# Fourteen gather tiles instead of eight at the start of a talking-heads attention and feed-forward kernel

## The chip, the cores and the metric

The kernel runs on one core of a Trainium2 chip. The metric is the device time of one execution in microseconds (us). The program is built once; nothing is computed on the host. A core has five engines that run their own instruction streams in order and wait for one another by semaphores: TensorE (PE, matrix products; PEld in a profile is its weight load), VectorE (DVE), ScalarE (ACT), GpSimd (POOL) and SyncE (SP, which here only issues transfers). Sixteen DMA engines move data; transfers are issued from the queues of SP, ACT and POOL.

## The reference

Inputs are q, k, v of shape 8 batches x 12 heads x 448 positions x 64, two 12 x 12 matrices that mix heads before and after the softmax, and two feed-forward weights (768 x 2048 and 2048 x 768).

```python
scores = scale * np.matmul(q, k.transpose(0, 1, 3, 2))
scores = np.einsum('bhij,hg->bgij', scores, w_pre)
attn = np.exp(scores - np.max(scores, axis=-1, keepdims=True))
attn = attn / (np.sum(attn, axis=-1, keepdims=True) + 1e-09)
attn = np.einsum('bhij,hg->bgij', attn, w_post)
out = np.matmul(attn, v)              # to 3584 rows x 768
h = np.maximum(out @ w_in, 0.0)
return (h * h @ w_out).astype(np.float32)
```

## The kernel before

**Stages.** For each batch, q and k are loaded into a staging tile (`load_third`, L78, three thirds of q and three of k), turned on PE and copied to `qT` and `kT` (`turn_unit`, L157). `score_pair` (L306) computes the scores of two heads for a block of 128 query rows; ACT casts one head and DVE the other into the block's tile `S` (L320), of which there are three. A block is two "halves" of 64 rows; a batch has seven halves. `half_of` (L300) says which half a query row lies in, `halves` (L303) which halves a block has. With the "+1" of L301 block 0 holds one half (rows 0 to 63 of batch 0), block 1 the next two, and so on.

**Gather.** To mix heads, PE needs heads on the partitions. `gather` (L333) copies ten queries of all twelve heads from `S` into a gather tile `G` (120 rows of 448 numbers, 105 KB) with one DMA, or two where the ten queries lie in two blocks. There are 45 such steps for a batch, 360 in all, and eight tiles `G` (L129), used in turn (L337). The transfers go out on SP's queue, but for steps 1 and 3, which go out on ACT's.

**The main loop** (L487) takes two steps at a time; it is called a double step here, numbered `ds` from 0 to 179. In one double step: `mix(ds)` (L348) multiplies the two gather tiles by `pre`, ACT takes the exponential and its row sums (L359), DVE the reciprocal (L361), POOL scales to `d` (L363). Two double steps later (`LAG`) `unmix` (L374) multiplies by `post` with 32 small products and DVE casts to `at` (L391). `scores_for` (L465) issues one or two score pairs, as far ahead as `AHEAD` + `LEAD` say, and `gathers_for` (L474) issues gathers up to step 2 ds + 8. `spin` (L410) is products without use that run in the first ten double steps.

**Feed-forward.** `av_unit` (L175) multiplies the attention by v and writes `xt`. `ffn1_unit` (L229) makes `h_ps` from `xt` and the first weights; then a rectifier writes `hr` and a square writes `h2`. Batches after the first go through with all 448 columns at once, rectified on ACT and squared on POOL. Batch 0 goes in three parts of 160, 160 and 128 columns (L517 to L519); there every odd unit is rectified and squared on DVE, and every even one on ACT and POOL (L242 to L246). `hr` has two buffers. `ffn2_unit` (L261) multiplies by the second weights and stores. These units are filler: they are put between the mixes of later double steps by `fill` (L401), and what is left after the last mix runs at the end.

**Loads.** All loads are issued from POOL's queue, in front of the `d` of a certain double step (`at_load`, L430; the number is in steps, so half of it is the double step). Before the loop: q and k of batch 0, a quarter of `w1` and half of v of batch 0. Then the rest of `w1` in double steps 1 to 4, q and k of batch 1 in 4 to 9, the eight pieces of `w2` (four tiles `w2_0` to `w2_3`, two pieces each) in 10 to 17, v of batch 1 in 22 and 23, q and k of batch 2 in 23 to 28. In the built program a load waits for the semaphore of the eighth load before it, and a gather for that of the eighth gather before it: there are eight semaphores for each kind.

The order on PE and POOL is that of the program text (`manual_schedule`, L420).

Of the kernel before, what the change touches and what calls it, by code (L numbers as in the profile page):

```python
# [9 lines left out]
BF16 = mybir.dt.bfloat16  # L10
F32 = mybir.dt.float32
ACT = mybir.ActivationFunctionType
# [3 lines left out]
B, H, S, D = 8, 12, 448, 64  # L16
DMODEL = H * D
DFF = 2048
NPAIR = H // 2
FT = DFF // 128  # L20
R = 7
PR = S // R
# [8 lines left out]
LAG = 2  # L31
AHEAD = 6
LEAD = 14
OFF = 64 - H * (IQ // 2)
SCALE = 1.0 / 8.0
FIRST_TURN = (15, 16, 17)
# [6 lines left out]
def kernel(  # L43
# [11 lines left out]
    nc = tc.nc  # L55
    P = nc.NUM_PARTITIONS

    consts = ctx.enter_context(tc.tile_pool(name="consts", bufs=1))
    wts = ctx.enter_context(tc.tile_pool(name="wts", bufs=1))
# [6 lines left out]
    def bank(name, dtype=F32):  # L66
        return psp.tile([P, 512 if dtype == F32 else 1024], dtype, name=name, tag="ps")
# [29 lines left out]

    col_pre = wcol(w_pre, "col_pre", nc.sync, (OFF, 64))
    col_post = wcol(w_post, "col_post", nc.scalar, (0, 64))

    def stripes(name, p0s):
        t = consts.tile([P, HQ], F32, name=name)
        for p0, c0 in zip((0, 64), p0s):
# [4 lines left out]

    stripe_pre, stripe_post = stripes("stripe_pre", (OFF, 64)), stripes("stripe_post", (0, 64))
    pre = consts.tile([P, 64], BF16, name="pre")  # L110
    nc.vector.memset(pre[:, :], 0.0)
    nc.vector.tensor_tensor(out=pre[:, 0:HR].rearrange("p (i g) -> p i g", g=H),
                            in0=stripe_pre[:, :].unsqueeze(2).to_broadcast([P, HQ, H]),
# [12 lines left out]
    for t in dts:  # L126
        nc.vector.memset(t[:, S:DW], 0.0)

    gts = [work.tile([P, S], BF16, name=f"G{x}") for x in range(AHEAD + 2)]  # L129
    for t in gts:  # L130
        nc.vector.memset(t[0:OFF, :], 0.0)

    attn = [atp.tile([P, VS, H, TW], BF16, name=f"at{x}") for x in range(2)]
    for t in attn:
# [3 lines left out]
    cgblk = consts.tile([P, NPAIR], F32, name="cgblk")  # L138
    wpost_bf = consts.tile([H, H], BF16, name="wpost_bf")
    w1 = [wts.tile([P, NPAIR, DFF // 4], BF16, name=f"w1_{x}") for x in range(4)]  # L140
    w2 = [wts.tile([P, FT // 4, DMODEL], BF16, name=f"w2_{x}") for x in range(4)]

    qTs, kTs, bvecs, xts, h2ts, ats = {}, {}, {}, {}, {}, {}

# [78 lines left out]
    def load_w2(x):  # L223
        n = DFF // 8
        c = x % 2 * 2
        nc.gpsimd.dma_start(out=w2[x // 2][:, c:c + 2, :],
                            in_=moe_w_out[n * x:n * x + n, :].rearrange("(c p) m -> p c m", p=P))

    def ffn1_unit(b, ft, half, c0=0, c1=S):  # L229
        if half == 0:  # L230
            h_open[0] = bank("h_ps")
        ps = h_open[0]
        n = c1 - c0
        for c2 in range(3 * half, 3 * half + 3):
            nc.tensor.matmul(ps[:, 0:n], lhsT=w1[ft // 4][:, c2, ft % 4 * 128:ft % 4 * 128 + 128],  # L235
                             rhs=xts[b][:, c2, c0:c1], start=(c2 == 0), stop=(c2 == NPAIR - 1))
        if half == 0:
            return
        if (b, ft) not in h2ts:
            h2ts[(b, ft)] = ffnp.tile([P, S], BF16, name="h2", tag="h2", bufs=FT + 1)  # L240
        hr = ffnp.tile([P, S], F32, name="hr", tag="hr", bufs=2)
        if n < S and ft % 2:  # L242
            nc.vector.tensor_scalar_max(out=hr[:, 0:n], in0=ps[:, 0:n], scalar1=0.0)
        else:
            nc.scalar.activation(out=hr[:, 0:n], in_=ps[:, 0:n], func=ACT.Relu)  # L245
        square = nc.vector if n < S and ft % 2 else nc.gpsimd  # L246
        square.tensor_tensor(out=h2ts[(b, ft)][:, c0:c1], in0=hr[:, 0:n], in1=hr[:, 0:n], op=ALU.mult)  # L247

# [49 lines left out]
    Sb, Gs, dsb = {}, {}, {}  # L298

    def half_of(b, c):  # L300
        return R * b + c // PR + 1  # L301

    def halves(n):  # L303
        return [(z, *divmod(2 * n + z - 1, R)) for z in range(2) if 0 <= 2 * n + z - 1 < R * B]

    def score_pair(i):  # L306

# [22 lines left out]
    def needs(s):  # L330
        return NPAIR * (span_of(s)[1] + 1)

    def gather(k):  # L333

        b, t = steps[k]
        c, end = IQ * t, min(IQ * t + IQ, S)
        g = gts[k % len(gts)]  # L337
        eng = nc.scalar if k in (1, 3) else nc.sync
        row = OFF
        while c < end:  # L340
            n, z = divmod(half_of(b, c), 2)
            x = PR * z + c % PR
            m = min(end - c, P - x)
            eng.dma_start(out=g[row:row + H * m, :], in_=Sb[n][x:x + m, :, :])
            c, row = c + m, row + H * m
        Gs[k] = g
# [72 lines left out]
    steps = [(b, t) for b in range(B) for t in range(NT)]  # L419
    with tc.manual_schedule(engines={PE, POOL}):  # L420
# [9 lines left out]
        def at_load(i, f, *args):  # L430
            loads.setdefault(i, []).append(lambda: f(*args))
# [2 lines left out]
            at_load(-1, load_w1, x)  # L434
        for x in range(4):
            at_load(-1 if x < 2 else 2, load_v, 0, x)
            at_load(44 + x, load_v, 1, x)
        for x in range(2, 8):
            at_load(1 + x, load_w1, x)
        for x in range(6):  # L440
            at_load(9 + 2 * x, load_qk, 1, x)
            at_load(46 + 2 * x, load_qk, 2, x)
        for x in range(8):
            at_load(20 + 2 * x, load_w2, x)
        for b in range(1, B):
            if b + 2 < B:
                for x in range(6):
# [5 lines left out]
        issued, gathered = [NPAIR + 3], [0]  # L453
# [5 lines left out]
        def place(tile):  # L459
            blk = sum(tile >= x for x in starts) - 1  # L460
            if blk + 1 >= blocks:
                return NPAIR * blocks
            return NPAIR * (blk + (tile - starts[blk]) / (starts[blk + 1] - starts[blk]))

        def scores_for(ds, most):  # L465
            want = math.ceil(place(2 * ds + AHEAD + LEAD))
            full = sum(gathered[0] >= x for x in lasts)
            want = min(want, issued[0] + most, NPAIR * min(full + 3, blocks))
            want = max(want, needs(steps[min(2 * ds + 4, len(steps) - 1)]))
            while issued[0] < want and all(issued[0] % NPAIR < turned.get(x[1], 0) for x in halves(issued[0] // NPAIR)):  # L470
                score_pair(issued[0])
                issued[0] += 1

        def gathers_for(ds):  # L474
            while gathered[0] < min(2 * ds + AHEAD + 2, len(steps)):
                if issued[0] < needs(steps[gathered[0]]):
                    break
                gather(gathered[0])
                gathered[0] += 1
# [7 lines left out]
        for ds in range(nd + LAG):  # L487
            for i in (2 * ds, 2 * ds + 1):
                for f in loads.get(i, []):
                    f()  # L490
            now2 = steps[2 * ds:2 * ds + 2]
            old2 = steps[2 * (ds - LAG):2 * (ds - LAG) + 2] if ds >= LAG else []
            for b, t in now2:
                if t == 0:
                    if b == 0:
                        at_step(ds + 6, (100, cg_unit))
                    if b + 1 < B:
                        for x in range(3):
                            turns[ds + TURN.get(b, TURN[B])[x]] = (b + 1, x)
            rest = ((NT + 1) // 2 + LAG + 2 - ds) % (NT / 2) + 1  # L500
            if EARLY[2] < ds <= EARLY[2] + 2:
                rest = NT // 2
            elif ds <= EARLY[2]:
                rest = 1 + min(x for x in EARLY if x >= ds) - ds
            share = sum(w for w, _ in filler) / rest if now2 else 1e9
            now = timed.pop(ds, [])
            for w, f in now:
                f()
            if old2:
                unmix(ds - LAG)  # L510
                for b1, t1 in old2:
                    ends = PARTS[b1 % 2]
                    if t1 + 1 in ends:
                        part = ends.index(t1 + 1) - 1
                        for x, u in enumerate(av_units(b1, part)):
                            at_step(ds + (2 + x if b1 else 1), u)
                        if b1 == 0:  # L517
                            c = (IQ * ends[part], min(IQ * ends[part + 1], S))
                            at_step(ds + 1, (0, lambda c=c: filler.extend(ffn1_units(0, *c))))  # L519
                    if t1 == NT - 1:  # L520
                        if b1 > 0:
                            at_step(ds + 3, (0, lambda b1=b1: filler.extend(ffn1_units(b1))))
                        at_step(ds + (3 if b1 else 1), (0, lambda b1=b1: filler.extend(ffn2_units(b1))))
            if ds in turns:
                turn_unit(*turns.pop(ds), (nc.vector.tensor_copy, nc.scalar.copy))
                scores_for(ds, 0)
            else:
                behind = place(2 * ds + AHEAD + LEAD) - issued[0]
                scores_for(ds, 2 if behind > (2 if now else 1.5) else 1)
            if now2:  # L530
                mix(ds)
            gathers_for(ds)
            if ds < PARTS[0][1] // 2 + LAG:
                spin(4)
            if ds + 1 < nd + LAG:
                fill(share)
# [34 lines left out]
```

## Time and profile before

| what | us |
|---|---|
| median of 7 runs | 606.64 |
| lowest, highest of them | 603.52, 610.35 |
| the profiled execution's own time | 604.29 |
| its span, first to last instruction | 602.5 |
| PE busy in the span | 545.1 (90%) |
| DVE busy | 415.2 (69%) |
| ACT busy | 404.5 (67%) |
| POOL busy | 400.2 (66%) |
| exponentials of double step 3 start at | 32.68 |
| of double step 17 | 79.17 |
| of double step 31 | 123.37 |
| of double step 179, the last | 547.11 |

Times inside an execution count from the span's start. Two exponentials belong to each double step, so counting them in the timeline of ACT tells which double step runs when. The table's last four rows are read that way. From double step 31 to 179 one takes 2.86 us on average (423.74 / 148); from 3 to 17 it takes 3.32 us (46.49 / 14), from 17 to 31 it takes 3.16 us (44.20 / 14). After the last mix some 55 us of feed-forward are left. In every profile a line such as `G<-S` is named by the program's tiles: written from read.

### The profile page before, as it was taken

The page shows a single profiled execution, that of the slowest core. Times are in us where ns is not written, and L with a number is a line of the kernel's source. Part 1 is how long each engine was busy: PE and PEld are TensorE (multiplying, and loading weights), DVE is VectorE, ACT ScalarE, POOL GpSimd, SP SyncE. Part 2 cuts the span into 40 slices and gives each one's busy share as a digit, 9 for nine tenths or more (in the row PEclk, how much of TensorE's full clock was granted, in tenths as well). Part 3 has the DMA queues.
Part 4 walks back from the last instruction along what each step waited for, and adds up shares of the span by engine and source line. Part 5 has one row for each costly group of instructions (what it writes and reads, how often), then busy time and mean ns, then how long its engine had stood idle before and what let it go on. Part 6 is the DMA issues. An engine that isn't in the chain of part 4 may idle for free.

```text
span 602.5 us, 28176 instructions
## 1 busy us (share of the span) xinstructions
PE 545.1 (90%) x11810; PEld 308.8 (51%) x11810; DVE 415.2 (69%) x1068; ACT 404.5 (67%) x1199; POOL 400.2 (66%) x599
## 2 busy tenths in 40 slices
PE   3667688888999999999999999999999999999997
PEld 1434455654455456545555455545555555555554
DVE  5646689978786777776877677667877787755101
ACT  3546477677688867886678767876788767862420
POOL 5465758857559964798459954897468946882450
PEclk9879999999999999999999999999999999999999
DMA  9799967949755895479646885489553765442103
GB/s 141 118 220 181 200 130 123 188 62 196 153 123 114 147 158 127 98 129 150 144 105 104 150 162 114 89 149 152 126 114 68 123 151 122 77 80 58 37 10 83
DMA packets 83364, 74.98 MB, mean 124 GB/s; under 512 B 6436, under 2 KB 80164, under 8 KB 83236
## 3 DMA queue, kind: packets, MB, share of 16 engines
q1 hardware_dynamic: 51582, 49.35, 35.4%
q0 software_dynamic: 31264, 23.60, 29.2%
q8 instruction: 92, 1.51, 1.0%
q10 hardware_dynamic: 390, 0.22, 0.1%
q14 instruction: 36, 0.29, 0.1%
HBM read 47.20 MB, written 11.01 MB: 97 GB/s over the span
## 4 chain that ended last, share of the span: by engine, by line
PE 64%; DMA 11%; POOL 10%; DVE 6%; ACT 3%; issue 3%; ACTq 0%; DVEq 0%
PE o_ps L268 22%; PE h_ps L235 18%; DMA G<-S 11%; PE at_ps L386 8%; PE ot_ps L186 6%; PE m_ps L354 5%; POOL d L363 4%; POOL h L247 4%; DVE at L391 3%; PE s_ps L316 3%; POOL qkst L70 2%; PE tr_ps L169 2%; ACT e_sb L359 1%; ACT xt L197 1%; DVE h L247 1%
## 5 line engine op out<-in xcount | busy, mean ns | idle before, releaser
L363 POOL TENSOR_SCALAR d<-e_sb,rc 128x448 bf16<-128x448 f32 x360 | 226.5, 640 | 161.2 <-DVE rc L361 159.1
L391 DVE CAST at<-at_ps 128x480 bf16<-128x480 f32 x360 | 220.0, 651 | 54.6 <-PE at_ps L386 49.6
L359 ACT ACTIVATE e_sb<-m_ps 128x448 f32<-128x448 f32 x360 | 195.3, 556 | 39.4 <-PE m_ps L354 28.3
L235 PE MATMUL h_ps<-xt,w 128*128 128x448 bf16 (+2 forms) x960 | 163.0, 316 | 3.9 <-DVE at L391 2.7
L268 PE MATMUL o_ps<-w,h 128*128 128x384 bf16 (+1 forms) x1024 | 161.6, 328 | 0.1
L247 POOL TENSOR_TENSOR h<-hr 128x448 bf16<-128x448 f32 (+2 forms) x136 | 113.7, 844 | 17.1 <-ACT hr L245 17.1
L235 PEld LDWEIGHTS <-w 128*128 128x128 bf16 x960 | 79.0, 97 | 79.2 <-issue 30.1
L268 PEld LDWEIGHTS <-h 128*128 128x128 bf16 (+1 forms) x1024 | 82.4, 101 | 70.8 <-issue 25.4
L320 ACT CAST S<-s_ps 128x448 bf16<-128x448 f32 (+1 forms) x174 | 90.9, 539 | 38.2 <-PE s_ps L316 35.9
L354 PE MATMUL m_ps<-G,pre 64*64 64x448 bf16 x720 | 84.8, 358 | 28.4 <-DMA G<-S 21.7
L320 DVE CAST S<-s_ps 128x448 bf16<-128x448 f32 (+1 forms) x174 | 104.6, 614 | 0.1
L361 DVE RECIPROCAL rc<-sm 128x1 f32<-128x1 f32 x360 | 53.3, 158 | 64.8 <-ACT e_sb L359 61.9
L386 PEld LDWEIGHTS <-d 60*64 60x64 bf16 x5760 | 65.3, 109 | 56.3 <-issue 30.9
L386 PE MATMUL at_ps<-post,d 60*64 60x60 bf16 x5760 | 86.4, 195 | 7.9 <-POOL d L363 4.1
L245 ACT ACTIVATE hr<-h_ps 128x448 f32<-128x448 f32 (+2 forms) x136 | 68.3, 511 | 23.8 <-PE h_ps L235 13.0
L359 ACT ACTIVATION_READ_ACCUMULATOR e_sb<-m_ps 128x1 f32 x360 | 77.8, 216 | 0.0
L197 ACT ACTIVATE xt<-ot_ps,bvec 128x160 bf16<-128x160 f32 (+3 forms) x144 | 44.5, 385 | 46.8 <-PE ot_ps L186 36.3
L316 PE MATMUL s_ps<-kT,qT 64*64 64x448 bf16 x672 | 64.0, 364 | 0.3 <-ACT qT L173 0.2
L354 PEld LDWEIGHTS <-pre 64*64 64x64 bf16 x720 | 29.6, 106 | 49.4 <-issue 38.6
L275 DVE COPY osb<-o_ps 128x384 f32<-128x384 f32 x48 | 26.0, 548 | 39.3 <-PE o_ps L268 39.1
L186 PE MATMUL ot_ps<-at,v 128*64 128x160 bf16 (+4 forms) x1152 | 45.8, 230 | 1.4 <-DVE at L391 1.4
L186 PEld LDWEIGHTS <-v 128*64 128x64 bf16 x1152 | 38.4, 109 | 14.5 <-issue 13.8
(41 smaller groups left out, 215.4 us busy)
## 6 DMA issues: line engine op xcount, KB each, us to landing
G<-S SPq DMA_DIRECT2D x330, 105.0 KB
out_dram<-osb SPq DMA_DIRECT2D x48, 192.0 KB
v<-in_v_dram POOLq DMA_DIRECT2D x32, 192.0 KB, 5.4
qkst<-in_k_dram POOLq DMA_DIRECT2D x24, 224.0 KB, 6.0
qkst<-in_q_dram POOLq DMA_DIRECT2D x24, 224.0 KB, 5.9
w<-in_moe_w_in_dram POOLq DMA_DIRECT2D x8, 384.0 KB, 11.5
w<-in_moe_w_out_dram POOLq DMA_DIRECT2D x8, 384.0 KB, 7.7
out_dram<-osb SPq DMA_DIRECT2D x16, 96.0 KB
```

Of the source, the lines that this page charges most:

```text
L186: nc.tensor.matmul(ps[64 * hh:64 * hh + 64, TW * y + c0:TW * y + 2 + n], lhsT=vs[b][:, g, r, :], rhs=at[:, r, g, c0:2 + n], start=(y == 0 ...
L235: nc.tensor.matmul(ps[:, 0:n], lhsT=w1[ft // 4][:, c2, ft % 4 * 128:ft % 4 * 128 + 128], rhs=xts[b][:, c2, c0:c1], start=(c2 == 0), stop=( ...
L245: nc.scalar.activation(out=hr[:, 0:n], in_=ps[:, 0:n], func=ACT.Relu)
L247: square.tensor_tensor(out=h2ts[(b, ft)][:, c0:c1], in0=hr[:, 0:n], in1=hr[:, 0:n], op=ALU.mult)
L268: nc.tensor.matmul(dst, lhsT=h2ts[(b, ft)][:, mt * 128:mt * 128 + ROWS[mt]], rhs=w2[ft // 4][:, ft % 4, n2 * 384:(n2 + 1) * 384], start=(f ...
L316: nc.tensor.matmul(pss[hh][PR * z:PR * z + PR, 0:S], lhsT=qTs[b][rs, p, PR * j:PR * j + PR], rhs=kTs[b][rs, p, :], start=True, stop=True)
L320: copy(out=Sb[n][z0:z1, 2 * p + hh, :], in_=pss[hh][z0:z1, 0:S])
L354: nc.tensor.matmul(pss[y][64 * x:64 * x + 64, 0:S], lhsT=pre[rows, :], rhs=gs[x][rows, :], start=True, stop=True)
L359: nc.scalar.activation(out=e[:, :], in_=pss[y][:, 0:S], func=ACT.Exp, scale=SCALE, accum_out=sm[:, 0:1])
L363: nc.gpsimd.tensor_scalar(out=d[:, 0:S], in0=e[:, :], scalar1=rc[:, 0:1], scalar2=-1.0 / S, op0=ALU.mult, op1=ALU.add)
L386: nc.tensor.matmul(us[x][PR * z:PR * z + PR, c:c + HR], lhsT=d[rows, j:j + PR], rhs=post[rows, :], start=True, stop=True)
L391: nc.vector.tensor_copy(out=dst, in_=src)
```

## The change

Six more gather tiles are used for the first 28 steps. They are slices of the room in which the last quarter of the second weights (`w2_3`) is loaded later; the tile that the loads write is a second one of the same name and room. `gather_tile` picks the tile of a step, `gather_end` says how far gathers are issued: up to step 2 ds + 14 at first, up to step 36 in double steps 11 to 14, and up to 2 ds + 8 as before from then on. The score pairs follow `gather_end`.

The halves are numbered anew: block 0 now holds the first two halves of batch 0, so that the first twelve gathers read block 0 alone; half 7 is left empty, so that block 3 holds one half and all later blocks are as before. The number of score pairs is the same (174).

v of batch 1 is loaded in double steps 18 and 19, q and k of batch 2 in 20 to 25. The pieces of `w2` stay in double steps 10 to 17. All rectifiers run on ACT; the squares of the odd units of batch 0 stay on DVE.

```diff
+MORE = 6
+HEAD = 2 * (AHEAD + 2 + MORE)
...
+    shared = wts.tile([P, FT // 4 * DMODEL], BF16, name="w2_3", tag="w2_3", bufs=1)
     gts = [work.tile([P, S], BF16, name=f"G{x}") for x in range(AHEAD + 2)]
-    for t in gts:
+    more = [shared[:, S * x:S * x + S] for x in range(MORE)]
+    for t in gts + more:
         nc.vector.memset(t[0:OFF, :], 0.0)
+
+    def gather_tile(n):
+        if n < HEAD:
+            n = n % (AHEAD + 2 + MORE)
+            return more[n - AHEAD - 2] if n >= AHEAD + 2 else gts[n]
+        return gts[(n - HEAD) % (AHEAD + 2)]
+
+    def gather_end(ds):
+        return min(2 * ds + AHEAD + 2 + MORE, max(HEAD + AHEAD + 2, 2 * ds + AHEAD + 2))
...
-    w2 = [wts.tile([P, FT // 4, DMODEL], BF16, name=f"w2_{x}") for x in range(4)]
+    w2 = [wts.tile([P, FT // 4, DMODEL], BF16, name=f"w2_{x}") for x in range(3)]
...
+        if x == 6:
+            last = wts.tile([P, FT // 4 * DMODEL], BF16, name="w2_3", tag="w2_3", bufs=1)
+            w2.append(last[:, :].rearrange("p (c m) -> p c m", m=DMODEL))
...
-        if n < S and ft % 2:
-            nc.vector.tensor_scalar_max(out=hr[:, 0:n], in0=ps[:, 0:n], scalar1=0.0)
-        else:
-            nc.scalar.activation(out=hr[:, 0:n], in_=ps[:, 0:n], func=ACT.Relu)
+        nc.scalar.activation(out=hr[:, 0:n], in_=ps[:, 0:n], func=ACT.Relu)
...
-        return R * b + c // PR + 1
+        return R * b + c // PR + (b > 0)
...
-        return [(z, *divmod(2 * n + z - 1, R)) for z in range(2) if 0 <= 2 * n + z - 1 < R * B]
+        return [(h % 2, *divmod(h - (h > R), R)) for h in (2 * n, 2 * n + 1) if h != R and h <= R * B]
...
-        g = gts[k % len(gts)]
+        g = gather_tile(k)
...
-            at_load(44 + x, load_v, 1, x)
+            at_load(36 + x, load_v, 1, x)
...
-            at_load(46 + 2 * x, load_qk, 2, x)
+            at_load(40 + 2 * x, load_qk, 2, x)
         for x in range(8):
-            at_load(20 + 2 * x, load_w2, x)
+            at_load(21 + 2 * x, load_w2, x)
...
-            want = math.ceil(place(2 * ds + AHEAD + LEAD))
+            want = math.ceil(place(gather_end(ds) + LEAD - 2))
...
-            while gathered[0] < min(2 * ds + AHEAD + 2, len(steps)):
+            while gathered[0] < min(gather_end(ds), len(steps)):
...
-                behind = place(2 * ds + AHEAD + LEAD) - issued[0]
+                behind = place(gather_end(ds) + LEAD - 2) - issued[0]
```

## The prediction

> **What bounds the kernel now.** I read the page first, then the chain of waits in the opening, then the DMA queues and the engines stretch by stretch.
>
> ```profile
> span 602.5 us, 28176 instructions
> ...
> PE   3667688888999999999999999999999999999997
> ...
> DMA  9799967949755895479646885489553765442103
> ...
> PE 64%; DMA 11%; POOL 10%; DVE 6%; ACT 3%; issue 3%; ACTq 0%; DVEq 0%
> ```
>
> The first rows are busy tenths in 40 slices of 15 us. From the eleventh slice on PE is at 9, so there the end is set by PE's work, and neither its amount nor its order there changes: in the built program the products on PE stand in the same order from double step 31 on. Only the first 123 us, where PE has digits from 3 to 8, can give or lose time; whatever is gained by double step 31 (exponentials at 123.37) moves all the rest. DMA's digits are highest in just that part, and the chain has 11% of DMA, 66 us. The chain from 20 to 80 us says where:
>
> ```profile
> by line: DMA G<-S 80.4%; PE spin_ps L416 6.3%; PE m_ps L354 5.4%; PE h_ps L235 3.1%; issue 3.0%; PE at_ps L386 2.3%; PE s_ps L316 1.8%; PE tr_ps L169 1.1%; PE ot_ps L186 1.0%; ACT e_sb L359 0.7%; ACT hr L245 0.3%
> ...
> 26.96 9.15 DMA G<-S
> ...
> 37.63 11.35 DMA G<-S
> ...
> 50.31 10.76 DMA G<-S
> ...
> 63.12 11.97 DMA G<-S
> ```
>
> Each piece is one gather, from its issue to its landing; the first took 4.99 us (16.82 to 21.8). So gathers queue. In the two queues' shares (packets, MB, share of 16 engines), first in 18 to 24 us, when hardly a load runs, then in 25 to 61 us:
>
> ```profile
> q1 hardware_dynamic: 561, 0.47, 36.3%
> q10 hardware_dynamic: 260, 0.22, 12.3%
> ```
>
> ```profile
> q0 software_dynamic: 5010, 4.40, 80.2%
> q1 hardware_dynamic: 2728, 2.26, 24.2%
> ```
>
> q1 and q10 are the gathers of SP and ACT: 0.69 MB in 6 us, 1.07 tiles of 107.5 kB a us. Beside the loads (q0) it is 2.26 MB in 36 us, 0.58 tiles a us: 3.4 us for the two tiles of a double step, and the steps take 3.32. A piece of 11.35 us at 0.58 a us means 6.6 tiles waiting out of eight, so the gather queue is always full and the DMA engines are the limit, not the issue. Before that stretch SP itself stood still once:
>
> ```profile
> L344 SPq EVENT_SEMAPHORE  x3: 17/17/2072, 16.8 to 25.8; - x3
> ```
>
> 2.07 us between 22.0 and 24.17: the second part of gather 6 waits for the casts of block 1 (DVE S is the releaser), with all later gathers behind it in SP's queue and the DMA engines idle. The stages, columns us, PE, PEld, DVE, ACT, POOL busy, clock, DMA share, GB/s:
>
> ```profile
> 20.00:79.17 59.17, 39.98 (x1097) 26.93 (x1098) 36.71 (x98) 32.08 (x99) 39.32 (x62) 0.91 0.99 186
> 79.17:123.37 44.20, 36.78 (x1039) 26.45 (x1037) 40.51 (x108) 32.71 (x105) 31.76 (x56) 1.00 0.75 138
> 123.37:547.00 423.63, 410.50 (x9048) 222.41 (x9047) 316.07 (x803) 319.69 (x959) 304.56 (x447) 1.00 0.65 124
> ```
>
> In the second stage DVE is busy 40.51 of 44.20 us, 92%: it is the bound there. In the third PE has 97%.
>
> **The change, part by part.**
>
> *Block 0 full, more tiles: the head start.* The first twelve gathers now need block 0 alone. Its six pairs cost the same casts (one per head, 448 columns, 64 or 128 rows: 624 and 617 ns on DVE between 12 and 20 us), and eight products of full blocks took PE 0.72 us at 17.73 where four of the half block took 0.94 at 11.32, so gather 0 goes out at 16.82 as now. SP issues one each 0.87 us (16.82, 17.70, 18.56, 19.42; one takes 1.60), so gather 11 goes out at 16.82 + 9 x 0.87 + 0.8 = 25.4, where it goes out at 28.77 now. The cap of eight semaphores does not bite: gather 8 at 22.8 waits for gather 0, landed at 21.8. Loads start at 24.36 and move from about 26 on. By then about 6.7 tiles are moved now (6.4 issued before SP's stall, little after it); after, what goes out by 24.3, gathers 0 to 9, so 10. A lead of 3.3 tiles at 0.58 to 0.62 a us (0.62 is 24 tiles over the 39 us between the landings at 36.1 and 75.1) is worth 5.3 to 5.7 us. It lasts as long as loads and gathers share the engines. Lower end: if the engines only do the same work in another order, a tile is worth its packets, 126 x 51 ns / 16 = 0.40 us, 3.3 tiles 1.3 us. Upper end: the first double steps run at 2.2 us (22.23 to 26.68 for two); at that pace double step 6 comes at 35.6 where it is 43.23: 7.6 us. I take 5.5, nearest to the measured rate.
>
> *Fourteen deep afterwards.* At most eight are in flight, by the semaphores, and 6.6 wait already, so the depth as such buys nothing while loads run: 0. If the rate did grow with depth, POOL's queue would be next: the load of double step 9 waits for the eighth load before it, issued at 30.53 and of a kind (`w1`) that takes 13.1 us to land (median, 25 to 85 us): 43.6. `d` of double step 9 stands behind it, 53.74 now. So it is 10 us at most; 0 at least.
>
> The Trainium skill ("DMA: Bandwidth & Descriptors", section "Queues, rings and completion order") says that each DMA engine takes turns between the queues that have work, packet by packet. By it a longer gather queue gets no larger share, and this part is worth nothing; without it, up to 10 us. The rate of 0.58 at a backlog of six agrees with it.
>
> *Rectifiers to ACT.* In the second stage DVE has 17 of them:
>
> ```profile
> L243 DVE TENSOR_SCALAR hr<-h_ps 128x160 f32<-128x160 f32 x10 | 3.1, 310 | 0.1
> ...
> L243 DVE TENSOR_SCALAR hr<-h_ps 128x128 f32<-128x128 f32 x7 | 2.0, 282 | 0.1
> ```
>
> DVE falls to 40.51 - 5.1 = 35.4. ACT's own take 314 and 284 ns, so ACT rises to 32.71 + 17 x 0.30 = 37.8 and becomes the longest, with PE at 36.78. If ACT is then as full as DVE now (92%) the stage takes 41.2: 3.0 us gained. Upper end 44.2 - 37.8 = 6.4. Lower end: a rectifier waits for its buffer, two squares back, and the next exponentials stand behind it on ACT, with reciprocal, `d` and `unmix` after them. The trace shows such waits:
>
> ```profile
>   ACT hr L245: 2.9, 4
> ```
>
> 0.73 us each, four times. If each of the stage's 35 rectifiers waited so, ACT would need 37.8 + 25.6 = 63.4, 19 us more than now. I take 3.0: at 1.2 units a double step the square two back has well over one double step to be done. The 7 rectifiers before 79 us lie in a stage that waits for gathers: 0.
>
> *Loads brought forward.* v of batch 1 moves four double steps, q and k of batch 2 three. POOL issues the same ten (0.65 to 0.7 us each). Now the DMA engines idle from 85 to 97 us (share 0.26) and gathers 45 on start alone there, after the casts of batch 1; then these loads and the end of `w2` run beside them. At 0.58 instead of 0.91 tiles a us (0.49 MB in 92 to 97) eight tiles take 5.0 us longer; but the same contention ends that much sooner behind them. Ends 0 and 5.0 lost; I take 0.5. The gain of keeping it is that the last third of q and k lands before the turn at double step 30, now issued at about 112 and used at 122.
>
> *At no cost.* Six memsets of 245 ns on DVE lie before its wait of 1.47 us for `col_pre`, and without that cover they would put off `kT` by 1.5 at most. The load into `w2_3` waits for gathers that landed three double steps before. Block 3's casts are as many as block 1's half was. Score pairs are skipped in double steps 11 and 12 and made earlier; ACT and DVE had room there.
>
> Sum: -5.5 - 3.0 + 0.5 = -8.0 on 604.29: 596.3. The median of the runs shown is 2.35 above that execution, so 598.6.
>
> **Rivals.**
> *The lead is given back (A).* Loads are tied to double steps; if they come as much earlier as the gathers, `w2`'s packets meet more backlog (0.69 tiles a us from 61 to 85 us) and only the 1.3 us of idle time is won, with 1 us of DVE. For it: DMA share 0.99 over the whole first stage. Against: after 85 us there is idle DMA to pay from. 606.64 - 2.3 = 604.3.
> *Gathers stop being the bound (B).* 10 + 5 = 15 us: 591.6. Against it the full queue at eight.
> *ACT's buffer wait (C), the slower side.* As above: +19 - 5.5 = +13.7, 620.3. It decides from a mean wait of (44.2 + 5.5 - 37.8) / 35 = 0.34 us a rectifier on. Against: now four of 48 wait.
> *The tiles do not act:* with the cap of eight only the 2.07 us stall goes, and with 2.5 of DVE's it is 602.1; it lies in the forecast's own range.
>
> **How the numbers follow.** Forecast 0.60, A 0.18, B 0.12, C 0.10. The predicted time is the forecast's, 598.6, own range 594 to 603. The range for 8 in 10 takes in A's and half of B's: 591 to 606. About 0.5%, 3 us, is what a measurement can tell: faster than 603.6 are the forecast but 0.01, B, and a quarter of A: 0.75. Within: the rest of A, 0.15. Slower: C, 0.10.
>
> **What would show it.** Right: gather 11 issued near 25.4 and no stall of 2 us on SP; double step 6 near 37.5, 17 near 74, 31 near 115.5; pieces of G still 10 us or longer up to 70 us; ACT the busiest engine from double step 17 to 31. Wrong: double step 17 at 78 or later (A) or before 68 (B), or waits of ACT hr on DVE h in dozens (C). It would also be wrong if the stretch after double step 31 changed from 479 us.

## The result and the profile after

| | before | after |
|---|---|---|
| median, us | 607.39 (36 runs) | 603.12 (15 runs) |
| lowest to highest | 603.52 to 610.94 | 600.41 to 605.17 |
| ratio of after to before, 95% interval | | 0.9926 [0.9907, 0.9944] |
| the profiled execution and its span | 604.29, 602.5 | 601.05, 599.3 |

The change gains 4.3 us by the medians, 0.7% by the ratio. It was put at 8.0: 598.6 was predicted, 603.1 came. First the rows of the page after that answer to those shown of before: PE, then the clock, then DMA in slices of 15 us.

```profile
span 599.3 us, 28171 instructions
...
PE   3876789888999999999999999999999999999996
...
PEclk9879699999999999999999999999999999999999
DMA  9899999559655885489556885489544765442102
...
PE 65%; DMA 12%; POOL 10%; DVE 4%; ACT 3%; issue 2%; SPq 1%; ACTq 0%; DVEq 0%
```

From the eleventh slice on PE is at 9 as before, so the gain lies ahead of it. DMA's share of the chain did not fall (12% against 11%). The clock row has a 6 in the fifth slice, 60 to 75 us; more of that below. The chain of waits from 20 to 80 us (start, length, what):

```profile
by line: DMA G<-S 43.8%; DMA w<-S 33.7%; SPq L357 11.4%; PE h_ps L251 3.1%; issue 3.0%; PE ot_ps L199 2.4%; PE m_ps L367 1.7%; PE at_ps L399 1.3%; PE tr_ps L182 1.1%; PE spin_ps L429 1.0%; PE s_ps L329 0.3%
...
25.52 8.65 DMA w<-S
...
34.23 11.29 DMA G<-S
...
47.11 11.55 DMA w<-S
...
58.73 15.00 DMA G<-S
```

`w<-S` are gathers too: those that write the six slices in the room of `w2_3`, which the program calls `w`. So gathers are 77.5% of this chain (80.4% before), and the last piece has grown from 11.97 to 15.00 us. SP's gather issues from 16 to 27 us (count, shortest/median/longest in ns, first and last start):

```profile
L357 SPq DMA_DIRECT2D G<-S x6: 768/821/2553, 16.6 to 22.8; - x6
L357 SPq DMA_DIRECT2D w<-S x4: 885/904/918, 23.6 to 26.5; - x4
...
L357 SPq EVENT_SEMAPHORE  x1: 17/17/17, 16.6 to 16.6; - x1
```

SP's wait of 2.07 us is gone, and gather 11 leaves at 26.5; one issue of 2.55 us put it 1.1 behind the 25.4 of the forecast (in the other kernels with the new numbering the longest issue there took 1.5 to 2.1 us). The stages, cut at the exponentials of double steps 17, 31 and 179 (columns as before: us, PE, PEld, DVE, ACT, POOL busy, clock, DMA share, GB/s):

```profile
20.00:78.39 58.39, 42.65 (x1086) 28.67 (x1086) 35.68 (x93) 32.83 (x103) 39.07 (x62) 0.82 1.03 189
78.39:118.65 40.26, 35.87 (x1040) 26.26 (x1037) 34.73 (x90) 35.42 (x123) 31.71 (x56) 1.00 0.82 151
118.65:543.41 424.76, 411.49 (x9048) 223.07 (x9047) 316.12 (x803) 320.38 (x960) 304.54 (x447) 1.00 0.65 124
```

The stage up to double step 17 took 58.39 us from 20 on where it took 59.17; that up to 31 took 40.26 where it took 44.20; the rest is as it was. Of the forecast's signs, the end of SP's stall and pieces of gathers over 10 us came (from 34 us on; the one before took 8.65), and the second stage became 3.9 us shorter, where the rectifiers were to give 3.0. Gather 11 (26.5 against 25.4), double step 6 (40.0 against 37.5) and 31 (118.65 against 115.5) came late; PE, not ACT, is the busiest engine of the second stage; and double step 17 came at 78.39, where "at 78 or later" was the sign for rival A.

How the head start went can be followed in the starts of the exponentials (us from the span's start; counted in ACT's timeline):

| double step | before | after | gain |
|---|---|---|---|
| 3 | 32.68 | 28.47 | 4.2 |
| 12 | 61.55 | 57.73 | 3.8 |
| 14 | 69.35 | 66.87 | 2.5 |
| 17 | 79.17 | 78.39 | 0.8 |
| 31 | 123.37 | 118.65 | 4.7 |
| 179 | 547.11 | 543.41 | 3.7 |

It was there, and between double steps 12 and 17 it went.

### The profile page after: what moved, and what is told of

Read it like the earlier page. It is cut to its first block, busy times and chain, and to the rows that moved or that the text cites. A ratio compares the mean times of both kernels' runs of the same rounds, so it can differ in the third digit from the quotient of the medians.

```text
span 599.3 us, 28171 instructions
## 1 busy us (share of the span) xinstructions
PE 548.8 (92%) x11810; PEld 312.1 (52%) x11810; DVE 409.3 (68%) x1050; ACT 409.1 (68%) x1223; POOL 399.8 (67%) x599
## 4 chain that ended last, share of the span: by engine, by line
PE 65%; DMA 12%; POOL 10%; DVE 4%; ACT 3%; issue 2%; SPq 1%; ACTq 0%; DVEq 0%
PE o_ps L281 23%; PE h_ps L251 19%; DMA G<-S 8%; PE at_ps L399 8%; PE ot_ps L199 6%; PE m_ps L367 5%; POOL d L376 4%; POOL h L260 4%; DMA w<-S 3%; PE s_ps L329 3%; DVE at L404 2%; POOL qkst L72 2%; PE tr_ps L182 2%; SPq L357 1%; ACT xt L210 1%
## 5 line engine op out<-in xcount | busy, mean ns | idle before, releaser
L251 PEld LDWEIGHTS <-w 128*128 128x128 bf16 x960 | 80.2, 99 | 77.9 <-issue 28.8
L367 PE MATMUL m_ps<-G,pre 64*64 64x448 bf16 (+2 forms) x696 | 80.0, 358 | 15.4 <-DMA G<-S 9.7
L258 ACT ACTIVATE hr<-h_ps 128x448 f32<-128x448 f32 (+2 forms) x160 | 74.1, 483 | 22.1 <-PE h_ps L251 11.4
L367 PEld LDWEIGHTS <-pre 64*64 64x64 bf16 x720 | 29.4, 107 | 42.3 <-issue 32.1
```

The lines of the kernel that those rows point to most:

```text
L367: nc.tensor.matmul(pss[y][64 * x:64 * x + 64, 0:S], lhsT=pre[rows, :], rhs=gs[x][rows, :], start=True, stop=True)
```

## The experiments

All ratios are to the kernel before, measured beside each experiment, with 95% intervals; each row has a profiled execution, whose exponentials stand beside it ("ds 3" is double step 3). Single executions of one kernel differ by some us, so ratios decide about the total and the exponentials about where.

| kernel | ratio | median us | ds 3 | ds 12 | ds 17 | ds 31 |
|---|---|---|---|---|---|---|
| e1, before + rectifiers | 0.9979 [0.9951, 1.0008] | 607.63 | 34.59 | 62.40 | 78.28 | 124.27 |
| e2, after without rectifiers | 0.9945 [0.9917, 0.9974] | 603.37 | 28.31 | 57.09 | 77.71 | 122.56 |
| e3, after, late loads as before | 0.9943 [0.9918, 0.9968] | 604.22 | 29.93 | 58.06 | 78.30 | 123.21 |
| e4, after with eight tiles | 0.9921 [0.9892, 0.9950] | 603.35 | 28.49 | 57.19 | 77.43 | 119.59 |
| e5, after, `w2` spread | 0.9964 [0.9928, 1.0000] | 605.17 | 29.43 | 59.34 | 75.19 | 121.21 |
| e6, after, longer `spin` | 0.9946 [0.9907, 0.9985] | 604.08 | 27.62 | 57.51 | 77.24 | 120.86 |
| e7, before + halves renumbered | 0.9964 [0.9934, 0.9993] | 606.71 | 29.36 | 57.73 | 77.22 | 124.19 |
| e8, before + six tiles | 1.0014 [0.9982, 1.0047] | 608.81 | 34.91 | 63.18 | 81.50 | 129.06 |
| e9, after, loads evened out | 0.9838 [0.9796, 0.9880] | 597.91 | 28.63 | 55.13 | 72.29 | 116.13 |
| e10, e9 + longer `spin` | 0.9845 [0.9799, 0.9891] | 598.96 | 28.06 | 55.14 | 70.21 | 118.52 |
| e11, after once more | 0.9936 [0.9909, 0.9963] | 603.99 | 28.06 | 57.07 | 77.97 | 120.75 |
| e12, before once more | 1.0010 [0.9981, 1.0039] | 606.89 | 32.77 | 61.40 | 79.21 | 125.18 |

**e1 and e2: the rectifiers, alone and taken back.** The theory first held, after the result (Theory 1), was that the head start is worth nothing in the end and the rectifiers make the net gain. e1 puts them into the kernel before, e2 takes them out of the kernel after:

```diff
-        if n < S and ft % 2:
-            nc.vector.tensor_scalar_max(out=hr[:, 0:n], in0=ps[:, 0:n], scalar1=0.0)
-        else:
-            nc.scalar.activation(out=hr[:, 0:n], in_=ps[:, 0:n], func=ACT.Relu)
+        nc.scalar.activation(out=hr[:, 0:n], in_=ps[:, 0:n], func=ACT.Relu)
```

> The kernel before with all rectifiers on ACT and nothing else. Theory 1 (the head start of the gathers is given back by double step 17; the net gain is the rectifiers'): double step 17 at 79 us as before, 31 at 119 to 120 instead of 123.4, time ratio to before 0.993 to 0.995. Theory 2 (the rectifiers gain little; the gain between double steps 17 and 31 comes from the loads that were brought forward, or is the head start coming back): 31 at 122 or later, ratio 0.998 or more.

> The changed kernel with the rectifiers of odd units of batch 0 on DVE as before. Theory 1: the opening as in the changed kernel (double step 12 at 57.7, 17 at 78.4), then 31 at 122 to 123, ratio to before 0.998 to 1.000. Theory 2: 31 at 119 to 120, ratio 0.993 to 0.995.

e1 gained 0.2%, not told from no change, and e2 kept 0.55% of the 0.74. Theory 1 falls: the rectifiers are the smaller part, some 0.2% or 1.2 us from either side (0.9979; 0.9945 against 0.9926), a size that neither pair tells from nothing by itself. The profiled executions do not decide it: e2's double step 31, at 122.56, came where Theory 1 had it, though its ratio is that of Theory 2.

**e3: the late loads back where they were.**

```diff
-            at_load(36 + x, load_v, 1, x)
+            at_load(44 + x, load_v, 1, x)
-            at_load(40 + 2 * x, load_qk, 2, x)
+            at_load(46 + 2 * x, load_qk, 2, x)
```

> The changed kernel with v of batch 1 and q, k of batch 2 loaded in their old double steps. Theory 1: these loads are worth nothing either way, ratio to before 0.991 to 0.994 as the changed kernel's 0.9926, double step 31 at 118 to 120. Theory 2, in the form that the loads brought forward make the gain: 31 at 122, ratio 0.997 or more.

0.9943 against 0.9926 and, in the repeat e11, 0.9936: bringing them forward is worth 0.1 or 0.2%, less than the intervals. It did no harm. (Double step 31 of e3, at 123.21, is later than Theory 1 had it; the ratio is not.)

**e4, e7, e8: tiles and numbering apart.** e4 is the kernel after with `MORE = 0`. e7 is the kernel before with the two lines of numbering alone, e8 with the six tiles and `gather_end` alone.

```diff
-MORE = 6
+MORE = 0
```

```diff
-        return R * b + c // PR + 1
+        return R * b + c // PR + (b > 0)
...
-        return [(z, *divmod(2 * n + z - 1, R)) for z in range(2) if 0 <= 2 * n + z - 1 < R * B]
+        return [(h % 2, *divmod(h - (h > R), R)) for h in (2 * n, 2 * n + 1) if h != R and h <= R * B]
```

```diff
-        g = gts[k % len(gts)]
+        g = gather_tile(k)
...
-            while gathered[0] < min(2 * ds + AHEAD + 2, len(steps)):
+            while gathered[0] < min(gather_end(ds), len(steps)):
```

> The changed kernel with eight gather tiles for all steps; the new numbering of the halves, the loads and the rectifiers stay. Theory 1: the renumbering alone takes away the stall of SP, so half of the lead or more is there at double step 3 (29 to 30.5 instead of 32.7; 28.5 with 14 tiles), and since the lead is given back anyway by 17 (78 to 79), the ratio is that of the changed kernel, 0.992 to 0.994. If the six tiles earn something in the end, the ratio is 0.995 or more.

> The kernel before with the new numbering of the halves alone (block 0 full); eight tiles, old loads, old rectifiers. If the net gain is the head start by the renumbering, the ratio is 0.993 to 0.996, with double step 3 at 28.5 to 30 (32.7 before). If the three parts only act together, it is 0.998 or more.

> The kernel before with the six more gather tiles and the gathers issued further ahead alone; old numbering, loads and rectifiers. SP's stall on block 1 stays. If depth is worth nothing beside the loads: double step 3 at 32 to 33 as before, ratio 0.998 to 1.001. If depth earns by itself: ratio 0.995 or less.

The six tiles, which give the change its name, are worth nothing that can be told: without them (e4) the ratio is 0.9921, and alone (e8) they gave 1.0014. The numbering alone (e7) makes the head start: double step 3 at 29.4, 12 at 57.7. And it alone loses most of it again by double step 17 (77.2); its ratio of 0.9964 is just short of the 0.993 to 0.996 that was expected. Over all profiled executions with `w2` where it was, double step 3 starts on average at 28.6 with the new numbering (after, e2, e3, e4, e6, e7, e11) and at 33.7 with the old (before, e1, e8, e12), a lead of 5.1; double step 12 at 57.5 and 62.1, 4.6; double step 17 at 77.8 and 79.5, 1.8. At double step 31 the averages are 121.4 and 125.5, but most of the kernels with the new numbering have the rectifiers and the loads of the change as well; e7, which has the numbering alone, is at 124.19 there, between the two executions of the kernel before (123.37 and 125.18), but that execution was a slow one (609.58 us where the median of e7 is 606.71). Whether some of the lead comes back stays open; the ratio of e7 says that 0.36%, 2.2 us, is kept in the end. Double step 3 of e8, at 34.91, is later than the 32 to 33 that was expected; so is that of e1, at 34.59, which has eight tiles.

**e5 and e6: where the lead goes.** From 60 to 72 us of the kernels before and after, the two queues' packets, MB and share of 16 engines (q0 the loads, here all `w2`; q1 the gathers):

```profile
q0 software_dynamic: 1083, 1.56, 80.9%
q1 hardware_dynamic: 1059, 0.88, 25.1%
```

```profile
q0 software_dynamic: 1083, 1.56, 79.2%
q1 hardware_dynamic: 772, 0.64, 20.4%
```

The same loads in both; gathers 0.88 MB before, 0.64 after. At 107.5 kB a tile that is 8.2 and 6.0 tiles in 12 us, 0.68 and 0.50 a us: 2.2 tiles fewer, 3.6 us at the 0.62 of the forecast. This is no chance of two executions: over these 12 us the four kernels with the old numbering (before, e1, e8, e12) moved 1035 to 1151 gather packets beside 1020 to 1100 of loads, the seven with the new one (after, e2, e3, e4, e6, e7, e11) 772 to 808 beside 1066 to 1183. Counted in single microseconds, gathers moved 56 to 97 packets in each of the twelve with the new numbering, with a median of 64 to 66; with the old numbering there are two to five microseconds among the twelve with 100 to 204. One of them is that from 62 to 63 us, first before, then after:

```profile
q0 software_dynamic: 83, 0.12, 65.1%
q1 hardware_dynamic: 167, 0.14, 42.8%
```

```profile
q0 software_dynamic: 84, 0.11, 81.2%
q1 hardware_dynamic: 67, 0.06, 21.4%
```

So what is lost with the new numbering is mainly these short stretches in which gathers go more than twice as fast. Two theories: the loads of `w2` take the lead away (W), or PE's half clock, which fell into the same stretch, does (C). e5 issues the pieces of `w2` every second double step, with v of batch 1 behind it; e6 keeps `spin` going up to double step 17, so that PE is seldom idle.

```diff
-            at_load(36 + x, load_v, 1, x)
+            at_load(52 + 2 * x, load_v, 1, x)
-            at_load(21 + 2 * x, load_w2, x)
+            at_load(21 + 4 * x, load_w2, x)
```

```diff
-            if ds < PARTS[0][1] // 2 + LAG:
+            if ds < 18:
```

> The changed kernel with the eight pieces of w2 loaded in every second double step (10, 12, ... 24) instead of 10 to 17, and v of batch 1 in 26 to 29. Theory W (the lead is lost in double steps 13 to 17 because gathers take turns with w2's long packets: 60 gather packets a us, 0.50 tiles, 4 us a double step): the gather rate from 60 to 72 us rises to 75 packets a us or more, double step 17 comes at 74 to 75.5 instead of 78.4, and if the later stages keep it, the ratio to before is 0.986 to 0.989. Theory C (the lead is lost to TensorE's clock, at half from 60.2 to 70.5 us): 17 stays at 77.5 to 79 wherever the clock is at half there, ratio 0.992 to 0.994.

> The changed kernel with the products without use (spin) kept up to double step 17 instead of 9. Theory C: no stretch at half clock between 50 and 80 us, double step 17 at 75 to 76.5, ratio to before 0.987 to 0.990. Theory W: the clock stays up, but double steps 13 to 17 still take 4 us each and 17 comes at 77.5 to 79; ratio 0.992 to 0.995.

The stretch from 60 to 70 us, first of the kernel after, then of e6 (columns as in the stages above; the clock is the third number from the end):

```profile
60.00:70.00 10.00, 7.75 (x185) 5.39 (x186) 4.37 (x12) 3.61 (x13) 6.26 (x11) 0.51 1.02 191
```

```profile
60.00:70.00 10.00, 6.78 (x227) 4.59 (x227) 5.30 (x14) 5.04 (x15) 6.40 (x11) 1.00 1.02 192
```

In e6 the clock is full, and the gathers (q1) from 60 to 72 us are about as slow as in the kernel after:

```profile
q1 hardware_dynamic: 808, 0.67, 21.0%
```

Double step 17 came at 77.24, where the other kernels with the new numbering have 77.22 to 78.39. So the half clock is not what takes the lead, and C falls for this stretch. In e5 the queues have, over the same 12 us:

```profile
q0 software_dynamic: 771, 1.07, 55.7%
q1 hardware_dynamic: 1233, 1.02, 27.5%
```

With 1.07 MB of loads instead of 1.56, 1.02 MB of gathers pass, and double step 17 is at 75.19, 2.6 ahead of the others, although the clock was at half from 60.8 to 67.6 us here too. That is W's mechanism: in six of the twelve microseconds the gathers of e5 move over 100 packets. The total was no better (0.9964), though: from there to double step 31 e5 took 46.0 us. In its chain from 75 to 122 us:

```profile
77.42 2.05 issue
...
84.39 1.34 issue
...
88.37 5.05 DMA G<-S
...
98.26 10.90 DMA G<-S
```

The loads put off are now met there: gathers are 16 us of the chain in a stage where ACT was to be the bound, and PE stood twice for over 1 us with nothing that the profile shows.

**e9 and e10: a schedule of loads that keeps the lead.** If it is loads in the gathers' way, then the early part of `w1` should move back too, since it is not needed in double steps 1 to 4, and what follows should be issued evenly. e9 does so, e10 adds `spin` up to double step 11.

```diff
-            at_load(-1 if x < 2 else 2, load_v, 0, x)
-            at_load(36 + x, load_v, 1, x)
+            at_load(-1 if x < 2 else 2 * x - 2, load_v, 0, x)
+            at_load(56 + 2 * x, load_v, 1, x)
...
-            at_load(1 + x, load_w1, x)
+            at_load((6, 8, 10, 12, 22, 24)[x - 2], load_w1, x)
...
-            at_load(9 + 2 * x, load_qk, 1, x)
-            at_load(40 + 2 * x, load_qk, 2, x)
+            at_load((14, 16, 18, 20, 23, 25)[x], load_qk, 1, x)
+            at_load(44 + 2 * x, load_qk, 2, x)
...
-            at_load(21 + 2 * x, load_w2, x)
+            at_load(28 + 2 * x, load_w2, x)
```

> The changed kernel with every load put off to about three double steps ahead of its use, at most one or two a double step (w1 in 3 to 12, q and k of batch 1 in 7 to 12, w2 in 14 to 21, q and k of batch 2 in 22 to 27, v of batch 1 in 28 to 31). If the burst of loads behind double steps 1 to 5 is what makes the gathers queue and gives the lead back: double step 12 at 51 to 54 instead of 57.7, 17 at 68 to 72, and part of it is left at 31 (112 to 117, 118.65 in the changed kernel), ratio to before 0.982 to 0.990. If the DMA work up to double step 31 is what counts, whatever its order, 17 is earlier but 31 stays at 118 to 121 and the ratio at 0.991 to 0.995.

> The same with the products without use kept for two more double steps (up to 11), where PE has least to do. If stretches at half clock after 45 us cost time there: 1 to 2 us less than the kernel with even loads alone. If they fall where PE waits for gathers anyway: the same ratio within 0.2%.

e9 gives 0.9838 [0.9796, 0.9880], 597.91 us, and beats both kernels: the repeat of the change beside it has 0.9936 [0.9909, 0.9963]. Double step 12 is at 55.13 and 17 at 72.29, a little short of what was expected of 12 and 17; the lead over the kernel before, 6.9 us at double step 17, is 7.2 at 31 and at 179. e9 moves every kind of load at once, so no run says which of them counts, and the even loads were not tried in the kernel before. Its first two stages:

```profile
20.00:72.29 52.29, 37.80 (x1079) 26.57 (x1080) 36.33 (x93) 33.08 (x103) 36.64 (x58) 0.91 0.99 180
72.29:116.13 43.84, 36.64 (x1046) 26.93 (x1043) 34.85 (x90) 34.75 (x122) 34.16 (x59) 0.99 0.90 168
```

DMA's share is 0.99 and 0.90 where the kernel after has 1.03 and 0.82: the engines' room after 78 us is used. The chain from 20 to 80 us now has a load in it:

```profile
by line: DMA G<-S 25.6%; DMA qkst<-in_q_dram 20.8%; POOL d L376 8.4%; PE spin_ps L429 6.6%; PE ot_ps L199 6.0%; PE h_ps L251 5.8%; DVE at L404 5.1%; PE at_ps L399 4.4%; PE s_ps L329 3.9%; POOL w L232 3.7%; issue 3.6%; PE m_ps L367 3.3%; PE 
...
35.81 10.65 DMA G<-S
...
56.98 12.48 DMA qkst<-in_q_dram
```

Gathers are 25.6% of this chain where they were 77.5, and the last third of q of batch 1, put off as well, sets the end of the stretch: it lands at 69.5, and PE's turn waits for it. That is the next thing to mend there; it was not tried. e10's longer `spin` made no difference that the ratio tells (0.9845).

**e11 and e12: both kernels once more.**

> The changed kernel once more, for a second profile and ratio. Ratio 0.990 to 0.995; double step 3 at 28 to 30, 12 at 57 to 58.5, 17 at 77 to 79, 31 at 118 to 122.

> The kernel before once more, for a second profile and as a measure of the noise. Ratio 0.998 to 1.002; double step 3 at 32.5 to 35, 12 at 61.5 to 63, 17 at 78.5 to 81.5, 31 at 123 to 126. If 17 came at 82 or later, the lead would be kept rather than given back.

0.9936 and 1.0010 agree with the first result and with no change. Their profiled executions show the same loss: 4.3 us at double step 12, 1.2 at 17 (61.40 and 79.21 against 57.07 and 77.97).

## Why the prediction was only half right

The time came within the 591 to 606 that was given, but between the forecast's 598.6 and rival A's 604.3.

**The bound: right.** The gather queue set the opening, and the stretch from double step 31 to 179 and on to the span's end takes 480.6 us after (479.1 before), so only the first 120 us gave anything.

**The head start, −5.5: sized right, its lasting wrong.** The lead of 3.3 tiles at 0.58 to 0.62 a us was to give 5.3 to 5.7 us; the averages of the profiled executions have 5.1 at double step 3 and 4.6 at 12. The step that failed is "It lasts as long as loads and gathers share the engines": it lasted to double step 12, and 1.8 was left at 17. By ratio the numbering alone (e7) gained 0.36%, 2.2 us. The rate of 0.62 a us, taken from the landings between 36 and 75 us of the kernel before, was carried on to gathers that meet `w2` at another point; there 0.50 was found. That 0.62 is an average which holds short stretches at twice the rate; with the new numbering they are missing from 60 to 72 us. That is rival A, "`w2`'s packets meet more backlog", for this term: its outcome came, and e5 and e9 show that the place of the loads decides it. What it does not say, and no run here tells, is why the same 1083 load packets leave such stretches with the old numbering (0.88 MB of gathers) and none with the new (0.64 MB); the clock (e6), the depth (e4) and the rectifiers (e7) are not the reason. A's price (1.3 us of idle time won) was near what the term kept.

**The depth, 0: right.** e4 and e8 agree. The cap of eight semaphores and the full queue were read rightly: between 16 and 84 us SP of the kernel after waited 25 times, 17.4 us in all, for a gather to land (by the rows below: total us, times, longest us), where that of e4, the same kernel with eight tiles, did so nine times, 5.5 us.

```profile
SPq L357 <- DMA G<-S: 9.3, 13, 1.2
SPq L357 <- DMA w<-S: 8.1, 12, 1.3
```

The Trainium skill ("DMA: Bandwidth & Descriptors", section "Queues, rings and completion order") has the engines take turns between queues, by which depth buys no share. These two runs agree with it.

**Rectifiers, −3.0: the load moved as forecast, the gain was put too high.** The two pairs say 0.2%, 1.2 us; their intervals reach from just below 0 to about 3, so 3.0 stands at their edge. DVE fell to 34.73 us in the second stage, as forecast (35.4), and ACT rose to 35.42, where 37.8 was worked out. But the 3.0 supposed that the stage is then as long as its fullest engine at 92%. In the kernel after, PE (35.87), ACT and DVE are all within 1.2 us of one another, and the stage takes 40.26; in e1 the same three are at 37.02, 35.42 and 34.74 and the stage takes 45.99, of which 2.4 us are one late double step (30; see the last section). Over the profiled executions with the new numbering the stage takes 40.3 to 44.9 us with the rectifiers on ACT (after, e3, e4, e6, e11) and 44.9 and 47.0 without (e2, e7), so single executions scatter by as much as the term. The stage's length does not follow its fullest engine; that waits pass between three engines of nearly equal load is the likely reason, which no run isolates.

**ACT's buffer wait (rival C): refuted.** In the view of the tile `hr` from 50 to 125 us, the row of ACT's own rectifiers among those who waited for it (us, times) is

```profile
  ACT hr L258: 0.8, 2
```

where before had 2.9 us in four. For 46 of the 48 rectifiers the square two back was done in time, as argued.

**Loads brought forward, +0.5: right in size, other sign** (e3: 0.1 to 0.2% gained, within its interval).

**Rival B** (gathers no longer the bound, 591.6) did not happen: the chain is gathers still. e9 shows what helps, and it is loads that move, not tiles. **"The tiles do not act"** is true of the tiles, and its 602.1 is the nearest of all to the result, in part by luck: it gave 2.07 us to the end of SP's stall, where the numbering first gained 5.1 and then kept 2.2, and 2.5 to the rectifiers, where 1.2 was measured.

The sum by what was measured: numbering 2.2, rectifiers 1.2, loads 0.4 to 1.0 (0.9943 against 0.9936 and 0.9926), tiles 0: 3.8 to 4.4, where the medians have 4.3. Each of these terms has an interval of about its own size, so the agreement proves little.

## What to carry to other kernels

Where gathers and loads share the DMA engines, as here, a head start of the gathers can be lost as soon as the next loads come due (5.1 us down to 1.8); plan the loads by when they are needed, evenly, and move back what is early (1.6% in e9), before adding buffers (nothing in e4 and e8). A rate measured in one stretch (0.62 tiles a us) holds for the loads that ran beside it, not for the next ones. Buffers beyond what can be in flight were worth nothing: look for the number of semaphores first.

## What the runs showed of the hardware

PE's clock fell to half in whole windows of 3.41 us, and not in the same places in two executions. In the kernel after, four windows of a grid of 3.41 us (columns as above):

```profile
56.80:60.22 3.42, 1.89 (x47) 1.22 (x46) 1.51 (x5) 1.66 (x6) 2.48 (x5) 1.00 1.15 204
60.22:63.63 3.41, 1.90 (x31) 1.05 (x16) 1.47 (x3) 0.84 (x4) 1.61 (x3) 0.50 1.05 187
...
145.56:148.97 3.41, 1.66 (x10) 0.82 (x11) 1.55 (x4) 1.47 (x5) 0.58 (x1) 1.00 1.05 190
148.97:152.38 3.41, 3.41 (x68) 2.28 (x65) 0.94 (x4) 1.11 (x5) 1.94 (x3) 0.50 0.69 171
```

A window in which PE was busy for 1.89 or 1.66 us of 3.41 (55 and 49%) is followed by one at clock 0.50. In the second case PE is full and pays at once: double step 41 to 42 takes 4.96 us where it takes 3.57 before, 1.39 lost, and the gain over before falls from 3.8 to 2.4 us in it. The Trainium skill ("TensorE: Matmul & The Clock Gate", Part 1, "The HAM clock gate (the "warmup" mystery)") has a free-running window of 3413 ns, which agrees with 3.41, and puts the half rate down to an idle window; here a window half busy could be enough. It was not always: in the kernel before, a window of 1.86 us busy is followed by one at full clock.

```profile
67.34:70.75 3.41, 1.86 (x79) 1.45 (x78) 1.32 (x6) 1.35 (x5) 1.79 (x4) 1.00 1.02 192
70.75:74.17 3.42, 2.44 (x128) 1.83 (x115) 2.75 (x9) 2.26 (x6) 2.47 (x5) 1.00 0.92 201
```

Counted over all fourteen profiled executions, from 15 to 190 us, in windows of each execution's own grid of 3.41 us that ran at full clock: with PE busy for less than 45% of the window, the next was at half clock in 28 of 28 cases; from 45 to 60%, in 29 of 61; from 60% on, in none of 507.

In e1 two half-clock windows in a row fell between the exponentials of double steps 30 and 32:

```profile
117.58:120.99 3.41, 1.74 (x43) 1.45 (x39) 2.71 (x7) 2.73 (x9) 1.99 (x4) 1.00 0.54 123
120.99:124.40 3.41, 2.13 (x78) 1.74 (x79) 1.73 (x3) 0.94 (x2) 0.76 (x3) 0.50 0.15 33
124.40:127.81 3.41, 3.41 (x51) 1.42 (x49) 2.17 (x7) 2.22 (x8) 1.28 (x2) 0.50 0.14 24
```

Its lead over before went from +1.5 us at double step 30 to −2.4 at 32. The clock is not all of that: in the chain of e1, PE stood still across the start of the first of the two windows, with nothing that the profile shows to wait for,

```profile
119.98 2.29 issue
```

and e4, at the same place in its program, has such a gap of 1.70 us at 115.90. What PE waits for there, no run tells. So late exponentials carry up to some us that belong to the execution and not to the kernel; the profiled execution of the kernel before, which shows no half clock in its span after 40 us, was a quick one (604.29 where the median is 607.39). A difference of some us in one execution is therefore read here as an effect only where several executions or a ratio bear it out.
